# Scores in two tiles, smaller first MLP chunks, and transposes moved from TensorE to DMA from block 12 on

## The chip, the cores and the metric

The kernel runs on one core of one Trainium2 chip. The metric is device time in microseconds (us). The engines are named as in the profile: PE (TensorE matmul), PEld (its weight load), DVE (VectorE), ACT (ScalarE), POOL (GpSimd) and SP (SyncE, whose queue issues most DMAs).

## The reference, cut to what matters

```python
# q, k, v: (8, 8, 576, 64) float32; w_ch1: (512, 2048), w_ch2: (2048, 512)
scores = q @ k.transpose / sqrt(64) - slope_h * |i - j|      # only 0 <= i - j < 128, else masked
x  = softmax(scores) @ v                                     # heads side by side: (8, 576, 512)
xn = (x - mean) / sqrt(var + 1e-6) * g_ln
out = x + relu(xn @ w_ch1) @ w_ch2
```

Attention looks back over at most 127 positions. The 8 x 576 rows of x then pass through a layer norm and a two-matmul MLP with a residual.

## The kernel before, in words

The 4608 rows form 36 blocks of 128 rows. Two sequences of 576 rows are nine blocks, so block number modulo 9 says where a block lies: r = 0 has no block before it, r = 4 is half one sequence and half the next.

**Attention of a block i.** SP loads q, k and v (three DMAs, or six where a block spans two sequences) into rings of five buffers. POOL casts them to fp16 (L337, L346). PE transposes q and k in eight 128x128 pieces into one PSUM bank (task `T`, L354), and DVE copies the bank to `qkt` (L362). PE makes the scores against this block's and the previous block's keys in two halves (`Sa` and `Sb`, L380), each a group of eight matmuls into its own half of one four-bank PSUM tile, `sc`. ACT takes the exponential of each half (L403), DVE multiplies it with a table of masks and biases (L409). PE multiplies with v (`pva`, `pvb`, L423), DVE divides by the row sums into `xb` (L439, L443), takes mean and variance (L459, L464) and makes `xs` (L470). PE transposes `xs` in four pieces (`TX`, L480), and ACT or DVE copies them into `xt` (L490, L488).

**MLP of a chunk.** Four blocks are a chunk. For each of 16 groups of hidden units PE does four matmuls of 512 columns into one PSUM bank (task `A`, L519), and ACT or DVE applies the relu (L531, L529). For each block 16 matmuls of 512 columns follow (task `B`, L545), DVE adds the residual (L553) and SP stores the block (L561). Four PSUM banks, `fb`, serve T, the value products, TX, A and B in turn.

**What sets the order.** Before anything is emitted, a planner (`Plan.run`) plays the program through with a cost for each task written into the code, and the order of each engine is the order in which the planner starts its tasks. Among tasks that could start at once it takes the one with the lowest due time `v`. Attention runs 1.45 chunks ahead of the MLP (`LEAD`). On the chip each engine runs its list in that order and waits on semaphores. SP's list mixes loads and stores. A new load may not be issued before the eighth DMA ahead of it on that queue has landed (the waits on DMAHW lanes in the order).

Of the kernel before, what the change touches and what calls it, by code (L numbers as in the profile page):

```python
# [45 lines left out]
class Plan:  # L46
# [17 lines left out]
    def run(self):  # L64
# [74 lines left out]
def kernel(  # L139
# [24 lines left out]
    NCHUNK = NBLK // CB  # L164
# [40 lines left out]
    q16 = ring("q16", 3, [P, d_model], FP16)  # L205
    k16 = ring("k16", 3, [P, d_model], FP16)
# [22 lines left out]
    LEAD = 1.45  # L229

# [15 lines left out]
    def dma(name, eng, issue, secs, emit, deps=(), v=0.0):  # L246
        t = add(name + ".i", (eng, issue), emit, deps, v, lat=0.0)
        return t, add(name, ("DMA", secs), None, [t], v, lat=2.0)
# [37 lines left out]
    for dst, lst, name in ((mmix, tmix, "mmix"), (mnew, tnew, "mnew")):  # L286
        vv = av(3, 0.0) - 200
# [10 lines left out]
    tmix += [add("z1", ("POOL", 0.6), z1, list(tmix), av(3, 0.1) - 200)]  # L298
    tmix += [add("z2", ("POOL", 0.6), z2, tmix[:2], av(3, 0.1) - 200)]
    tnew += [add("z3", ("POOL", 1.2), z3, list(tnew), av(3, 0.1) - 200)]  # L300
# [10 lines left out]
    W_AFTER = {0: 4, 1: 8}  # L311
    t_w1, t_w2 = [], []
    for n in range(4):
        def emit(e, b, n=n):
            nc.gpsimd.dma_start(out=w1sb[:, :, 512 * n : 512 * n + 512], in_=w1r[:, :, 512 * n : 512 * n + 512])
        t_w1.append(dma(f"w1_{n}", "POOL", 0.9, 3.25, emit, loads[W_AFTER[0] - 1][2], av(W_AFTER[0], 0.5) - 300)[1])
    for n in range(4):
        def emit(e, b, n=n):
            nc.gpsimd.dma_start(out=w2sb[:, 4 * n : 4 * n + 4, :], in_=w2r[:, 4 * n : 4 * n + 4, :])
        t_w2.append(dma(f"w2_{n}", "POOL", 0.9, 3.25, emit, loads[W_AFTER[1] - 1][2], av(W_AFTER[1], 0.5) - 300)[1])  # L320

    qkt_done, vx_done, aggr_done, xt_done = {}, {}, {}, {}

    def attention(i):
# [5 lines left out]
        def e_cast(dst, src):  # L330
            def emit(e, b):
                en = {"POOL": nc.gpsimd, "DVE": nc.vector}.get(e)
                s = src[i][:, :, :].rearrange("p h d -> p (h d)")
                if en is None:
                    nc.scalar.activation(out=dst[i][:, :], in_=s, func=AF.Copy)
                else:
                    en.tensor_copy(out=dst[i][:, :], in_=s)  # L337
            return emit

        c_eng = {"POOL": 0.62}  # L340
        cq = add(f"cq{i}", c_eng, e_cast(q16, q32), lq, av(i, 0.0))
        ck = add(f"ck{i}", c_eng, e_cast(k16, k32), lk, av(i, 0.1))
        q32.reads(i, cq); k32.reads(i, ck); q16.writes(i, cq); k16.writes(i, ck)

        def e_cv(e, b):
            nc.gpsimd.tensor_copy(out=vx[i][:, :, 0:D], in_=v32[i][:, :, :])  # L346
        cv = add(f"cv{i}", ("POOL", 0.66), e_cv, lv_, av(i, 0.2))
        v32.reads(i, cv); vx.writes(i, cv)

        def e_t(e, b):  # L350
            pt = fb[b][:, :].bitcast(FP16).rearrange("p (a hp c) -> p a hp c", a=2, hp=HP)
            for a, s in ((0, q16), (1, k16)):
                for hp in range(HP):
                    nc.tensor.transpose(pt[:, a, hp, :], s[i][:, hp * P : hp * P + P], iden[:, :])  # L354
        tt = add(f"T{i}", ("PE", 0.48), e_t, [cq, ck, d_iden], av(i, 1.0), acq=("fb", f"T{i}"))
        q16.reads(i, tt); k16.reads(i, tt)

        def e_ev(e, b):
            src = fb[plan.held[f"T{i}"][1]][:, :].bitcast(FP16)
            dst = qkt[i][:, :, :, :].rearrange("p a hp c -> p (a hp c)")  # L360
            if e == "DVE":
                nc.vector.tensor_copy(out=dst, in_=src)  # L362
            else:
                nc.scalar.activation(out=dst, in_=src, func=AF.Copy)
        ev = add(f"ev{i}", {"DVE": 0.7}, e_ev, [tt], av(i, 1.2), rel=f"T{i}")
        qkt.writes(i, ev)
# [4 lines left out]
        def e_s(half):  # L371
            def emit(e, b):
                for slot in range(2):
                    hp = 2 * half + slot
                    for side in (() if r == 0 else (0,)) + (1,):
                        for g in range(2):
# [4 lines left out]
                                sc[:, 2 * half + g, c0 : c0 + P],  # L381
# [5 lines left out]
            return emit  # L387
# [4 lines left out]
        for half, s_ in ((0, sa), (1, sb_)):  # L392
            qkt.reads(i, s_)
            if r:
                qkt.reads(i - 1, s_)

            def e_x(e, b, half=half):
                o = probs[i][:, 2 * half : 2 * half + 2, :, lo:]
                n_ = sc[:, 2 * half : 2 * half + 2, :].rearrange("p b (s c) -> p b s c", s=2)[:, :, :, lo:]
                if r:  # L400
                    o = o.rearrange("p b s c -> p b (s c)")
                    n_ = sc[:, 2 * half : 2 * half + 2, :]
                nc.scalar.activation(out=o, in_=n_, func=AF.Exp, scale=inv_sqrt_d)  # L403
            ex = add(f"ex{'ab'[half]}{i}", ("ACT", 1.03 if r else 0.62), e_x, [s_], av(i, 2.4 + half), rel=f"S{'ab'[half]}{i}")
            probs.writes(i, ex)

            def e_m(e, b, half=half):
                pv = probs[i][:, 2 * half : 2 * half + 2, :, lo:]
                nc.vector.tensor_tensor(out=pv, in0=pv, in1=mask[:, 2 * half : 2 * half + 2, :, lo:], op=ALU.mult)  # L409
            pr.append(add(f"mk{'ab'[half]}{i}", ("DVE", 0.69 if r else 0.42), e_m, [ex] + t_mask, av(i, 3.0 + half)))  # L410
# [45 lines left out]
        c, j = i // CB, i % CB  # L456
# [17 lines left out]
        xs_ = add(f"xs{i}", ("DVE", 0.69), e_xs, [ag, d_g], av(i, 6.6))  # L474
        xs.writes(i, xs_)

        def e_tx(e, b):
            pt = fb[b][:, :].bitcast(FP16)[:, 0 : NKB * P].rearrange("p (kb c) -> p kb c", kb=NKB)
            for kb in range(NKB):
                nc.tensor.transpose(pt[:, kb, :], xs[i][:, kb * P : kb * P + P], iden[:, :])  # L480
        tx = add(f"TX{i}", ("PE", 0.26), e_tx, [xs_, d_iden], av(i, 7.5), acq=("fb", f"TX{i}"))
        xs.reads(i, tx)

        def e_xt(e, b):
            src = fb[plan.held[f"TX{i}"][1]][:, :].bitcast(FP16)[:, 0 : NKB * P].rearrange("p (kb c) -> p kb c", kb=NKB)
            dst = xt[c][:, :, j * P : j * P + P]
            if e == "DVE":
                nc.vector.tensor_copy(out=dst, in_=src)  # L488
            else:
                nc.scalar.activation(out=dst, in_=src, func=AF.Copy)  # L490
        xt_ = add(f"xt{i}", {"ACT": 0.6, "DVE": 0.45}, e_xt, [tx], av(i, 7.6), rel=f"TX{i}")
        xt.writes(c, xt_)
        xt_done[i] = xt_

        if j == CB - 1:
            ag4 = [aggr_done[c * CB + n] for n in range(CB)]

            def e_ln(e, b):
                nc.scalar.activation(out=lv[c][:, :], in_=mv[c][:, :, 1], func=AF.Ln, bias=eps_t[:, :])
# [105 lines left out]
```

## Time and profile before

| | us |
|---|---|
| median of 3 runs | 363.4 (362.27 to 363.58) |
| the profiled execution, its own time | 362.91 |
| its span, first to last instruction | 361.1 |
| PE busy | 332.4 (92%) |
| DVE busy | 216.7 (60%) |
| ACT busy | 157.5 (44%) |
| POOL busy | 78.8 (22%) |

The median and the profiled execution's time are of the whole launch; the span is what the engines' records cover. Busy time of PE counts modelled ends of pipelined matmuls. The granted TensorE clock is 1.00 throughout.

### The profile page before, as it was taken

The numbers are of one execution on the slowest core, as the hardware profiler recorded it, in microseconds if no ns is written. First come the engines' busy times: TensorE is split into PE (matmuls) and PEld (weight loads), VectorE is DVE, ScalarE is ACT, GpSimd is POOL, SyncE is SP. The second block draws the span as 40 slices with busy tenths as digits, with TensorE's granted clock in tenths as the row PEclk, the third lists the DMA queues.
The fourth block names the chain that finished last, engine by engine and source line by source line (L and its number), as shares of the span: only waits on it lengthen the run. The fifth ranks groups of instructions, "written<-read, shape, count | busy, mean of one in ns | idle before, by whom it ended". The sixth has DMA issues, their size and how long they took to land.

```text
span 361.1 us, 6732 instructions
## 1 busy us (share of the span) xinstructions
PE 332.4 (92%) x2672; PEld 173.4 (48%) x2672; DVE 216.7 (60%) x444; ACT 157.5 (44%) x237; POOL 78.8 (22%) x127
## 2 busy tenths in 40 slices
PE   1586999999999999999999999999999999999995
PEld 0364455545545545544554554555455555444442
DVE  0578497667658666666657666765676667641011
ACT  4253576245334542464245433653365335612700
POOL 4851541632112121112101211230111100000000
PEclk9999999999999999999999999999999999999999
DMA  9999999999996444564454346441000010002002
GB/s 169 226 194 212 218 196 208 201 230 224 234 186 196 93 88 124 142 115 93 122 134 93 89 118 145 119 89 56 33 29 2 29 61 31 0 31 87 0 33 86
DMA packets 122384, 42.75 MB, mean 118 GB/s; under 512 B 113392, under 2 KB 117616, under 8 KB 122352
## 3 DMA queue, kind: packets, MB, share of 16 engines
q1 hardware_dynamic: 118128, 38.12, 47.0%
q0 software_dynamic: 4224, 4.19, 7.0%
q8 instruction: 21, 0.34, 0.4%
q14 instruction: 11, 0.09, 0.1%
HBM read 37.06 MB, written 9.44 MB: 129 GB/s over the span
## 4 chain that ended last, share of the span: by engine, by line
PE 80%; ACT 12%; DVE 3%; POOL 2%; DMA 1%; issue 1%; SPq 0%; ACTq 0%; DVEq 0%
PE fb L519 32%; PE fb L545 32%; ACT probs L403 8%; PE sc L380 5%; PE fb L423 5%; PE fb L354 4%; PE fb L480 2%; ACT xt L490 2%; ACT ht L531 1%; DMA k<-in_k_dram 1%; DVE probs L409 1%; DVE xb L443 1%; POOL mmix L290 1%; POOL mnew L290 1%; DVE st L459 1%
## 5 line engine op out<-in xcount | busy, mean ns | idle before, releaser
L519 PE MATMUL fb<-xt,w1sb 128*128 128x512 f16 x576 | 140.7, 383 | 0.0
L545 PE MATMUL fb<-w2sb,ht 128*128 128x512 f16 x576 | 137.7, 379 | 0.0
L531 ACT ACTIVATE ht<-fb 128x512 f16<-128x512 f32 x118 | 70.4, 598 | 75.3 <-PE fb L519 75.1
L403 ACT ACTIVATE probs<-sc 128x1024 f16<-128x1024 f32 (+1 forms) x72 | 69.8, 974 | 37.2 <-PE sc L380 36.9
L519 PEld LDWEIGHTS <-w1sb 128*128 128x128 f16 x576 | 51.3, 98 | 52.9 <-issue 1.4
L545 PEld LDWEIGHTS <-ht 128*128 128x128 f16 x576 | 51.0, 98 | 52.3
L553 DVE SCALAR_TENSOR_TENSOR ot<-fb,rstd,xb 128x512 f32<-128x512 f32 x36 | 26.8, 748 | 46.4 <-PE fb L545 45.3
L346 POOL CAST vx<-v 128x512 f16<-128x512 f32 x36 | 22.6, 631 | 137.7 <-PE fb L423 128.9
L409 DVE TENSOR_TENSOR probs<-probs,mreg 128x1024 f16<-128x1024 f16 (+1 forms) x56 | 37.2, 666 | 24.8 <-ACT probs L403 24.4
L423 PEld LDWEIGHTS <-probs 128*128 128x128 f16 x544 | 26.9, 102 | 20.4 <-DVE probs L409 3.5
L490 ACT ACTIVATE xt<-fb 128x512 f16<-128x512 f16 x20 | 11.9, 597 | 55.1 <-PE fb L480 52.2
L337 POOL CAST q<-q 128x512 f16<-128x512 f32 x36 | 23.5, 653 | 57.1 <-issue 25.1
L380 PEld LDWEIGHTS <-qkt 64*128 64x128 f16 x544 | 19.4, 98 | 31.8 <-issue 24.7
L423 PE MATMUL fb<-vx,probs 128*128 128x65 f16 x544 | 29.9, 200 | 4.4 <-POOL vx L346 3.1
L529 DVE TENSOR_SCALAR ht<-fb 128x512 f16<-128x512 f32 x26 | 18.0, 692 | 24.1 <-PE fb L519 24.1
L380 PE MATMUL sc<-qkt,qkt 64*128 64x128 f16 x256 | 23.0, 229 | 9.4 <-ACT probs L403 6.6
L443 DVE TENSOR_TENSOR xb<-fb,rec 128x256 f16<-128x256 f32 x72 | 30.3, 423 | 2.1
L362 DVE COPY qkt<-fb 128x1024 f16<-128x1024 f16 x36 | 24.7, 686 | 10.4 <-PE fb L354 10.3
L470 DVE SCALAR_TENSOR_TENSOR xs<-xb,mv,g_t 128x512 f16<-128x512 f16 x36 | 28.3, 787 | 1.0
L380 PE MATMUL sc<-qkt 64*128 64x128 f16 x288 | 25.3, 229 | 0.8 <-DVE qkt L362 0.8
L459 DVE BATCH_NORM_STATS2 st<-xb 128x6 f32<-128x512 f16 x36 | 25.0, 694 | 1.1
L337 POOL CAST k<-k 128x512 f16<-128x512 f32 x36 | 23.0, 640 | 8.1 <-DMA k<-in_k_dram 8.0
(28 smaller groups left out, 135.8 us busy)
## 6 DMA issues: line engine op xcount, KB each, us to landing
out_dram<-ot SPq DMA_DIRECT2D x36, 256.0 KB, 2.1
q<-in_q_dram SPq DMA_DIRECT2D x32, 256.0 KB, 4.3
k<-in_k_dram SPq DMA_DIRECT2D x32, 256.0 KB, 4.6
v<-in_v_dram SPq DMA_DIRECT2D x32, 256.0 KB, 4.4
w1sb<-in_moe_w_ch_dram POOLq DMA_DIRECT2D x4, 512.0 KB, 10.9
w2sb<-in_moe_w_ch_dram POOLq DMA_DIRECT2D x4, 512.0 KB, 11.0
q<-in_q_dram SPq DMA_DIRECT2D x8, 128.0 KB, 3.7
k<-in_k_dram SPq DMA_DIRECT2D x8, 128.0 KB, 3.6
```

The source lines that it names most:

```text
L337: en.tensor_copy(out=dst[i][:, :], in_=s)
L380: nc.tensor.matmul(sc[:, 2 * half + g, c0 : c0 + P], kt[rows, 1, hp, :], qkt[i][rows, 0, hp, :], start=True, stop=True,)
L403: nc.scalar.activation(out=o, in_=n_, func=AF.Exp, scale=inv_sqrt_d)
L409: nc.vector.tensor_tensor(out=pv, in0=pv, in1=mask[:, 2 * half : 2 * half + 2, :, lo:], op=ALU.mult)
L423: nc.tensor.matmul(pp[:, hh * (D + 1) : hh * (D + 1) + D + 1], probs[i][:, bank, slot, side * P : side * P + P], vx[i - 1 + side][:, h, 0 ...
L443: nc.vector.tensor_tensor(out=xb[i][:, 256 * half : 256 * half + 256].rearrange("p (h d) -> p h d", d=D), in0=pp[:, :, 0:D], in1=rec[2 * i ...
L459: nc.vector.bn_stats(out=st[i][:, :], in_=xb[i][:, :])
L470: nc.vector.scalar_tensor_tensor(out=xs[i][:, :], in0=xb[i][:, :], scalar=mv[c][:, j, 0:1], in1=g_t[:, :], op0=ALU.subtract, op1=ALU.mult,)
L519: nc.tensor.matmul(fb[b][:, :], w1sb[:, kb, f * P : f * P + P], xt[c][:, kb, :], start=(kb == 0), stop=(kb == NKB - 1),)
L531: nc.scalar.activation(out=ht[c][:, f, :], in_=src, func=AF.Relu)
L545: nc.tensor.matmul(pm[:, :], ht[c][:, f, j * P : j * P + P], w2sb[:, f, :], start=(f == 0), stop=(f == NFB - 1),)
L553: nc.vector.scalar_tensor_tensor(out=ot[i][:, :], in0=fb[plan.held[key][1]][:, :], scalar=rstd[c][:, j : j + 1], in1=xb[i][:, :], op0=ALU. ...
```

## The change

- **Transposes by DMA.** From block 12 on q and k are cast into one tile `qk16` (a ring of four in place of two rings of three), and one DMA transpose on SP's queue writes `qkt` from it (256 KB). `xs` is transposed by a second one into `xt` (128 KB). For these 24 blocks the PE tasks T and TX and the copies behind them are gone. Blocks 0 to 11 keep them.
- **Scores as one task.** `sc` becomes two tiles, `scs[0]` and `scs[1]`, and all 16 score matmuls of a block are one task `S`.
- **Chunks.** The first two MLP chunks have two blocks, the other eight have four.
- **The start.** The copies and memsets for the special mask tables get a later due time, and the eight pieces of the weights are asked for one by one after the loads of blocks 2 to 7, instead of in fours after blocks 3 and 7.
- **The planner.** It passes over an engine for a task that another engine would finish earlier, takes DMAs first come first served, and has some costs changed.

```diff
@@ Plan.run
-                    if r is not None:
-                        cand.append((max(r, f), t.v, t, b))
+                    if r is None:
+                        continue
+                    s = max(r, f)
+                    if any(max(r, free[o]) + c < s + t.eng[e] - 1e-9 for o, c in t.eng.items() if o != e):
+                        continue
+                    cand.append((s, t.v, t, b))
...
-                c = min((c for c in cand if c[0] <= s + 1e-9), key=lambda c: c[1])
+                c = min((c for c in cand if c[0] <= s + 1e-9), key=lambda c: (c[2].v > -9e3, c[2].ready) if e == "DMA" else c[1])
@@ the chunks and the score tiles
+    CHUNKS = [2, 2] + [4] * 8
+    FIRST = [sum(CHUNKS[:c]) for c in range(len(CHUNKS))]
+    CHUNK_OF = [c for c, n in enumerate(CHUNKS) for _ in range(n)]
...
-    q16 = ring("q16", 3, [P, d_model], FP16)
-    k16 = ring("k16", 3, [P, d_model], FP16)
+    qk16 = ring("qk16", 4, [P, 2, d_model], FP16)
...
-    sc = psum.tile([P, 4, 512], FP32, tag="sc", name="sc")
+    scs = [psum.tile([P, 2, 512], FP32, tag=f"sc{n}", name=f"sc{n}") for n in range(2)]
...
-    plan.banks["sa"] = [0]
-    plan.banks["sb"] = [1]
+    plan.banks["sc"] = [0]
...
+    QK_BY_DMA = 12
+    X_BY_DMA = 12
@@ masks and weights
-        vv = av(3, 0.0) - 200
+        vv = av(2, 3.0)
...
-    W_AFTER = {0: 4, 1: 8}
+    W_AFTER = [2, 2, 3, 3, 4, 5, 6, 7]
@@ attention(i): q and k
+        if i < QK_BY_DMA:
...
+        else:
+            def e_td(e, b):
+                nc.sync.dma_start_transpose(
+                    out=qkt[i][:, :, :, :].rearrange("p a hp c -> p (a hp) c"),
+                    in_=qk16[i][:, :, :].rearrange("p a d -> p (a d)"),
+                )
+            ti, ev = dma(f"QT{i}", "SP", 1.0, 1.1, e_td, [cq, ck], av(i, -4.0))
+            qk16.reads(i, ev)
+            qkt.writes(i, ti)
@@ attention(i): scores
-        sa = add(f"Sa{i}", ("PE", 0.38), e_s(0), [ev] + prev, av(i, 2.0), acq=("sa", f"Sa{i}"))
-        sb_ = add(f"Sb{i}", ("PE", 0.38), e_s(1), [sa] + prev, av(i, 2.0), acq=("sb", f"Sb{i}"))
+        s_ = add(f"S{i}", ("PE", 0.64 if r else 0.42), e_s, [ev] + prev, av(i, 2.0), acq=("sc", f"S{i}"))
@@ attention(i): the normalised x
+        if i < X_BY_DMA:
...
+        else:
+            def e_xd(e, b):
+                nc.sync.dma_start_transpose(out=xt[c][:, :, j * P : j * P + P], in_=xs[i][:, :])
+            xi, xt_ = dma(f"XT{i}", "SP", 1.0, 0.6, e_xd, [xs_], av(i, 7.0))
+            xs.reads(i, xt_)
+            xt.writes(c, xi)
```

The order on **PE** at the scores of one steady block. Before (`sc` is the one score tile, `qkt_98` a transposed q and k, `fb_153` a PSUM bank, block 18, which has no block before it and so four matmuls in each half):

```order
L380 LDWEIGHTS qkt_98
L380 MATMUL sc<-qkt_98 128x128
L519 LDWEIGHTS w1sb
L519 MATMUL fb_153<-xt_122,w1sb 128x512
L519 LDWEIGHTS w1sb
L519 MATMUL fb_153<-xt_122,w1sb 128x512
L519 LDWEIGHTS w1sb
L519 MATMUL fb_153<-xt_122,w1sb 128x512
L519 LDWEIGHTS w1sb
L519 MATMUL fb_153<-xt_122,w1sb 128x512
L380 LDWEIGHTS qkt_98
L380 MATMUL sc<-qkt_98 128x128 [waits Activation_49]
```

Now, block 16 (`sc_147` and `sc_148` are the two score tiles; eight matmuls go to each, and the last of the first and the first of the second are shown):

```order
L401 LDWEIGHTS qkt_94
L401 MATMUL sc_147<-qkt_94 128x128
L401 LDWEIGHTS qkt_97
L401 MATMUL sc_148<-qkt_94,qkt_97 128x128
L401 LDWEIGHTS qkt_97
L401 MATMUL sc_148<-qkt_94,qkt_97 128x128
```

The four wide matmuls between the halves are gone from there, and the second half no longer waits for ACT. The first score matmul of a block from 12 on waits for a DMA instead of DVE (`L401 MATMUL sc_147<-qkt_94,qkt_97 128x128 [waits DMAHW3_49]` in block 16).

The order on **SP** around the loads of block 17. Before (`q_72`, `k_77`, `v_82` are its load buffers; a DMAHW lane is the DMA eight places ahead):

```order
L561 DMA out_dram<-ot_130 128x512 [waits DMAHW7_49,DVE_49]
L254 DMA q_72<-in_q_dram 128x8x64 [waits DMAHW0_49,Pool_49]
L254 DMA k_77<-in_k_dram 128x8x64 [waits DMAHW1_49,Pool_49]
L254 DMA v_82<-in_v_dram 128x8x64 [waits DMAHW2_49,Pool_49]
L254 DMA q_73<-in_q_dram 128x8x64 [waits DMAHW3_49,Pool_49]
L254 DMA k_78<-in_k_dram 128x8x64 [waits DMAHW4_49,Pool_49]
```

Now (`qkt_94<-qk_85` is block 12, `qkt_95<-qk_86` block 13):

```order
L261 DMA q_72<-in_q_dram 128x8x64 [waits DMAHW0_49,Pool_49]
L261 DMA k_77<-in_k_dram 128x8x64 [waits DMAHW1_49,Pool_49]
L381 DMA_TRANSPOSE qkt_94<-qk_85 128x8x128 [waits DMAHW2_49,PE_49]
L261 DMA v_82<-in_v_dram 128x8x64 [waits DMAHW3_49,Pool_49]
L261 DMA q_73<-in_q_dram 128x8x64 [waits DMAHW4_49,Pool_49]
L261 DMA k_78<-in_k_dram 128x8x64 [waits DMAHW5_49,Pool_49]
L381 DMA_TRANSPOSE qkt_95<-qk_86 128x8x128 [waits DMAHW6_49,PE_49]
```

The transposes stand among the loads of five blocks later and wait for PE, which frees the `qkt` buffer. Ahead of block 12's stand 53 loads of 256 KB (counted in whole ones) and four stores.

The order on **POOL** at the start. Before (`vx_91<-v_80` is block 0's cast of v):

```order
L337 CAST q_85<-q_70 128x512 [waits DMAHW1_49]
L337 CAST k_88<-k_75 128x512 [waits DMAHW2_49]
L290 COPY mmix<-mreg 128x1024 [waits Activation_49] x2
L290 COPY mnew<-mreg 128x1024 x2
L293 MEMSET mmix 128x8x64 [waits Pool_49]
L295 MEMSET mmix 64x8x64
L297 MEMSET mnew 64x8x128 [waits Pool_49]
L346 CAST vx_91<-v_80 128x8x64 [waits DMAHW3_49]
```

Now (`vx_89<-v_80` is that cast):

```order
L344 CAST qk_85<-q_70 128x512 [waits DMAHW1_49]
L344 CAST qk_85<-k_75 128x512 [waits DMAHW2_49]
L297 COPY mmix<-mreg 128x1024 [waits Activation_49]
L357 CAST vx_89<-v_80 128x8x64 [waits DMAHW3_49]
L297 COPY mmix<-mreg 128x1024 [waits Activation_49]
L344 CAST qk_86<-q_71 128x512 [waits DMAHW5_49]
```

One of the seven mask steps is left ahead of the cast of v; the others lie between the casts of blocks 0 to 3.

More of the change, by code (lines that the diff above doesn't have):

```diff
@@ L355, in attention @@
[L355 to L365, printed above, removed]
@@ L367, in attention, with e_s @@
         qkt_done[i] = ev
         prev = [] if r == 0 else [qkt_done[i - 1]]
-        def e_s(half):
-            def emit(e, b):
+        def e_s(e, b):
+            for half in range(2):
                 for slot in range(2):
@@ L473, in e_xs @@
             )
-        xs_ = add(f"xs{i}", ("DVE", 0.69), e_xs, [ag, d_g], av(i, 6.6))
+        xs_ = add(f"xs{i}", ("DVE", 0.75), e_xs, [ag, d_g], av(i, 6.6))
         xs.writes(i, xs_)
[L477 to L492, printed above, removed]
+        xs_done[i] = xs_
@@ L514, in mlp @@
             key = f"A{c}.{f}"
[L515 removed]
+            vm = v0 + f * per
             def e_a(e, b, f=f):
@@ L566 @@
         attention(i)
-    for c in range(NCHUNK):
+    for c in range(len(CHUNKS)):
         mlp(c)
```

149 lines of the change are left out of this document (91 added, 58 removed).

## The prediction

> **What bounds the kernel now.** I read the page's busy table first, then the windows by stage, then the chain of waits inside the steady stage, then PE's own waits. The windows (columns after the stretch: PE, PEld, DVE, ACT and POOL busy, granted clock, DMA share, GB/s):
>
> ```profile
> span 361.1 us, 6732 instructions
> PE 332.4 (92%) x2672; PEld 173.4 (48%) x2672; DVE 216.7 (60%) x444; ACT 157.5 (44%) x237; POOL 78.8 (22%) x127
> ...
> 0.00:36.00 36.00, 18.74 (x199) 13.34 (x200) 20.63 (x53) 14.37 (x23) 18.35 (x31) 1.00 1.14 200
> 36.00:108.00 72.00, 69.84 (x600) 36.59 (x598) 48.36 (x99) 34.43 (x52) 25.69 (x39) 1.00 1.09 213
> 108.00:252.00 144.00, 140.27 (x1158) 72.28 (x1156) 95.56 (x193) 67.70 (x101) 27.76 (x46) 1.00 0.46 112
> ```
>
> From 36 us on PE is busy 97% of each stretch at full clock, and DVE reaches only two thirds, so PE sets the pace. The DMA engines are full until 108 us and half idle afterwards. That split matters below. The chain of waits through one steady block, and PE's timeline at the same place:
>
> ```profile
> 182.91 0.92 ACT probs L403
> ...
> 201.38 1.03 ACT probs L403
> 202.40 0.04 issue
> 202.44 0.40 PE sc L380 x8
> 202.84 1.83 PE fb L519 x8
> 204.67 0.24 PE fb L423 x8
> ...
> 206.89 0.45 PE fb L354 x8
> 207.33 2.59 PE fb L545 x12
> 209.92 0.24 PE fb L480 x4
> ...
> 220.09 0.92 ACT probs L403
> ```
> ```profile
> 200.78 0.23 PE L380 MATMUL sc<-qkt,qkt 64*128 64x128 f16 x2
> ...
> 201.10 1.04 PE L519 MATMUL fb<-xt,w1sb 128*128 128x512 f16 x4
> 202.44 0.23 PE L380 MATMUL sc<-qkt,qkt 64*128 64x128 f16 x2 [0.30 <-ACT probs L403]
> ```
>
> One exponential per block ends in the chain, and the rows at 182.91 and 220.09 lie four blocks apart: 37.18/4 = 9.30 us per block. What PE must do in one: 12 wide matmuls in 2.59 us are 0.216 us each, and a block has 32 of them (16 at L519, 16 at L545): 6.91. The eight q and k transposes (L354) 0.45, the four of x (L480) 4 x 0.056 = 0.22, two score halves at 201.10 - 200.78 = 0.32 each, two value halves at 0.24: 8.70 in all. So 0.60 us per block is lost. Most of it is one wait. The second score half follows four wide matmuls that begin at 201.10 and need 0.86, so it could start at 201.96. It starts at 202.44, when the first half's exponential is over: 0.48 us. The two halves lie in one tile, `sc`, and in the built order the second half waits for ACT.
>
> **The change part by part.** (a) *Twelve transposes leave PE in 24 blocks (12 to 35).* 24 x (0.45 + 0.22) = 16.1 us, all on PE's path. DVE's copies of the results to `qkt` and the copies to `xt` on ACT and DVE go too.
>
> ```profile
> L362 DVE COPY qkt<-fb 128x1024 f16<-128x1024 f16 x36 | 24.7, 686 | 10.4 <-PE fb L354 10.3
> L488 DVE COPY xt<-fb 128x512 f16<-128x512 f16 x16 | 6.8, 424 | 8.6 <-PE fb L480 8.6
> L490 ACT ACTIVATE xt<-fb 128x512 f16<-128x512 f16 x20 | 11.9, 597 | 55.1 <-PE fb L480 52.2
> ```
>
>  They ran under PE's wide matmuls, so they count for nothing here; uncovered they would be 0.69 and 0.42 to 0.60 us a block.
>
> (b) *Two score tiles, and one score step.* The scores now run as 16 matmuls with no wait between the halves. The exponentials run back to back on ACT, which is busy for 67.70 of 144 us, and PE has wide matmuls to fill in. The saving is 0.48 us each time. How often?
>
> ```profile
> PE 80%; ACT 12%; DVE 3%; POOL 2%; DMA 1%; issue 1%; SPq 0%; ACTq 0%; DVEq 0%
> PE fb L519 32%; PE fb L545 32%; ACT probs L403 8%; PE sc L380 5%; PE fb L423 5%; PE fb L354 4%; PE fb L480 2%; ACT xt L490 2%; ACT ht L531 1%; DMA k<-in_k_dram 1%; DVE probs L409 1%; DVE xb L443 1%; POOL mmix L290 1%; POOL mnew L290 1%; DVE st L459 1%
> ...
> PE sc L380 <- ACT probs L403: 6.6, 22, 0.6
> ```
>
> PE's waits record it 22 times. Eight per cent of the span is about 29 exponentials of 1 us in the chain. I take 27, since two or so lie in the start where other waits rule: 27 x 0.48 = 13.0 us, bounds 10.6 and 14.
>
> (c) *The start.* POOL's mask work of 5.8 us stands before the first cast of v, and PE's first value matmul waits 3.1 us for that cast. In the new order one mask copy is ahead of it. The first MLP chunk now needs two blocks instead of four, with the weights asked for earlier.
>
> ```profile
> 6.45 2.03 POOL L290 COPY mmix<-mreg 128x1024 f16<-128x1024 f16 x2
> 8.42 2.03 POOL L290 COPY mnew<-mreg 128x1024 f16<-128x1024 f16 x2
> ...
> 11.31 0.94 POOL L297 MEMSET mnew<- 64x1024 f16 x1
> 12.21 0.60 POOL L346 CAST vx<-v 128x512 f16<-128x512 f32 x1
> ...
> PE fb L423 <- POOL vx L346: 3.1, 1, 3.1
> ...
> 34.34 1.71 PE fb L519 x4
> ...
> 343.52 13.83 PE fb L545 x64
> 357.37 0.75 DVE ot L553
> ```
>
> Split into two halves, the first chunk has 64 more matmuls of half the width; at 0.108 us each they are still longer than the 0.056 at which the x8 row above passes matmuls with their own weights, so the sum stays. Counted over the program in these durations, PE has 1152 x 0.216 + 544 x 0.04 + 544 x 0.03 + 432 x 0.056 = 311 us of matmuls before, and with 144 transposes 295 after. So 361.1 - 311 = 50 us are lost now: the tail after 357.37 is 3.7, the stage 36 to 324 holds 31 blocks at 0.60 = 18.6, and about 27.7 fall in the first 36 us. The change can win back between nothing and about 10 of these. What caps it is (d).
>
> (d) *48 DMA transposes enter SP's queue*, in line with loads and stores: 256 KB per block for q and k, 128 KB for x; each issue holds SP for about as long as the load in the last row below, so six a block stay far below 8 us. No transposing DMA is in this trace. The nearest rows:
>
> ```profile
> q1 hardware_dynamic: 118128, 38.12, 47.0%
> q0 software_dynamic: 4224, 4.19, 7.0%
> ...
> out_dram<-ot SPq DMA_DIRECT2D x36, 256.0 KB, 2.1
> q<-in_q_dram SPq DMA_DIRECT2D x32, 256.0 KB, 4.3
> k<-in_k_dram SPq DMA_DIRECT2D x32, 256.0 KB, 4.6
> ...
> 105.63 0.37 SPq L254 DMA_DIRECT2D v<-in_v_dram  x1
> ```
>
> SP's queue moves 38.12 MB in 0.470 x 361.1 = 169.7 us, or 1.17 us per 256 KB. That is the lower bound: 1.17 + 0.58 = 1.75 us of the DMA engines per block. The upper bound is a load's whole landing time with no overlap, 4.6 + 2.3 = 6.9 us. I take 1.17 and 0.58 and add a little for gaps, because a square of 128 columns has rows of 256 bytes, as a head's row in a load has. The Trainium skill, DMA: Bandwidth & Descriptors, section "Latency and other measured facts", gives 261 GB/s for such a transpose, an estimate of 1.0 us for 256 KB; no run here shows it yet.
>
> When does this bind? In the order, the transpose for block 12 stands behind 53 loads, 4 stores and all weights: 57 x 1.17 + 0.07 x 361.1 (25.3) + about 1.6 for the small tables = 93.6, plus its own 1.17, a start at about 2 us and 0.9 to report (a store lands after 2.1, of which 1.17 is transfer): 97.7 us. PE, before it comes to block 12's scores, has 128 half-wide and 172 wide matmuls, 176 for scores, 176 for values and 144 transposes: 71.4 us. With today's 27.7 of lost start and 0.1 a block it is there at about 100. The two nearly meet, so a better start buys 2 or 3 us at most; above that PE would only wait for the transpose. The same tie holds up to block 19. After that the loads thin out (0.46 of the DMA engines' time above) and each transpose may be issued once the scores of three blocks earlier are done, some 24 us before its own, so a few us of delay hide. The x transposes have more: they feed MLP chunks, of which the first is that of blocks 12 to 15.
>
> The added wait: a transpose waits on PE for a free `qkt` buffer or on DVE for `xs`, and behind it in SP's queue stand the loads of five blocks later and stores. POOL's casts and then PE wait for those, late by the same amount. I add 1 to 8 us for late transposes between blocks 12 and 19, and take 4.
>
> *Sum.* 361.1 - 16.1 - 13.0 - 3 + 4 = 333.0. A second way: scores of block 12 at 99, then 223.6 us of matmuls, 24 x 0.1, a tail of 3.7 and the 4: 332.7. The profiled execution took 362.91 us beside its span of 361.1, so 1.8 is added: **334.5 us**. Its 362.91 lies 0.5 under the median of 363.4, which I leave alone.
>
> **The rivals.** *Late queue, still faster.* The tie of (d) goes against PE: each of the 8 + 4 transposes that fall while the queue is full costs a further 1 us, about a load's share of the engines once more, if SP's queue runs dry behind each. For it speak the DMA share of 1.09 up to 108 us and a median landing of 4.3 to 4.6 us for a load, four times its transfer. Against it: the engines have half their time free soon after. 334.5 + 12 = 346 us.
>
> *Slower.* Transposes do not overlap in the queue, and each holds it for its landing time: 6.9 us a block beside 3 loads and 1 store at 4.7. Then 24 x 11.6 = 278 us from 97.7 on, and after the last x transpose the last chunk remains (4 x 6.91 + 3.7 = 31.3): 407 + 1.8 = 409 us. It decides from where 24 x (4.7 + X) exceeds 361.1 - 97.7 - 31.3 = 232 us, at X = 5.0 us a block, 2.9 times the loads' rate. For it: the trace holds no such transfer, and SP's queue is one. Against it: a load lands after 4.6 us and costs 1.17, so about four are in flight in that queue at once.
> *Slower, square by square.* The 12 squares of 128x128 of a block pass one after another, each at half the landing time of the smallest plain table of two squares:
>
> ```profile
> dist_t<-dist SPq DMA_DIRECT2D x1, 64.0 KB, 1.7
> ```
>
> 12 x 0.85 = 10.2 us a block, so 97.7 + 24 x 14.9 + 31.3 + 1.8 = 488 us. Against it: that landing is mostly latency, since 64 KB at the loads' rate is 0.29 us. The Trainium skill's page VectorE: DVE Perf Modes, section "The three transpose paths", speaks for this rival and against the change: 1309 ns for a DMA transpose of 128x128, 390 ns on TensorE, and TensorE advised. By it, an estimate, a block has 15.7 us and the time is some 620 us. This trace disagrees on TensorE, where eight take 0.45 us in a row, so I read both figures as those of one transpose alone.
>
> *No gain.* The gain of (a) and (b) is eaten by another engine. DVE has 95.56 of 144 us and loses copies, and ACT has 67.70, so this needs a cause that I do not see; the time would stay near 363 us.
>
> **How the numbers follow.** Forecast, 326 to 343 us: 0.70. Late queue, 343 to 361: 0.16. Below 326, the start worth more: 0.02. Within 0.5% of 363.4, about what a measurement here can tell from no change: 0.02. Slower: 0.10, of which 0.08 by landing times and 0.02 square by square. The range 325 to 350 holds the forecast and most of the late queue, 0.82. Faster is 0.70 + 0.16 + 0.02 = 0.88.
>
> **What would show it.** (a) L354 and L480 fall to a third of their instructions. (b) No PE wait on the exponential between score halves, and a block period near 9.30 - 0.48 - 0.67 = 8.15 us after block 20. (c) The first L519 matmul well before 34.34 us. (d) Transposes of 256 KB that take 1 to 1.5 us of the DMA engines, and PE waits on DMA of under 8 us in all, between 95 and 145 us. The forecast is wrong if PE waits for transposes beyond block 20, or if SP's queue shows holds of several us at each of them.

## The result, and the profile after

The changed kernel takes **332.83 us** (median of 4 runs, 329.89 to 333.16) against 362.95 us (median of 4 runs, 362.27 to 363.58) for the kernel before: a ratio of 0.915, 95% interval 0.910 to 0.921. Medians and ratios are of fast runs alone; one run below, 338.39 us of the kernel with one score tile, is a slow one. Predicted were 334.5 us and a range of 325 to 350. The profiled execution took 333.16 us with a span of 331.4. The total is within 2 us; the terms of the sum are not all that near, and the experiments below take them apart.

The page of the changed kernel: span, busy times, queues (packets, MB, share of 16 DMA engines), chain by engine, and the last group of the transposes that stay on PE.

```profile
span 331.4 us, 6333 instructions
PE 306.1 (92%) x2448; PEld 162.3 (49%) x2448; DVE 194.6 (59%) x409; ACT 151.1 (46%) x242; POOL 81.3 (25%) x127
...
q1 hardware_dynamic: 156528, 47.56, 70.6%
...
PE 84%; DMA 5%; DVE 4%; POOL 3%; SPq 1%; issue 1%; ACT 0%; DVEq 0%
...
L366 PE MATMUL fb<-iden,qk 128*128 128x128 f16 x96 | 9.3, 254 | 7.4 <-DMA iden<-iden 7.3
```

PE is still 92% busy of a span that is 29.7 us shorter, so PE still sets the pace. ACT's 12% of the chain is gone. The q and k transposes on PE are 96 instead of 288. SP's queue carries 9.4 MB more, and its share of the engines went from 47.0% to 70.6%. PE's waits (total, times, longest, in us):

```profile
PE fb L366 <- DMA iden<-iden: 7.3, 1, 7.3
PE fb L503 <- DVE xs L491: 5.5, 3, 2.8
PE sc L401 <- DVE qkt L374: 2.8, 5, 0.9
PE fb L443 <- DVE probs L429: 2.2, 5, 0.9
PE fb L552 <- DMA w1sb<-in_moe_w_ch_dram: 0.8, 1, 0.8
PE fb L552 <- DVE xb L463: 0.7, 1, 0.7
PE sc L401 <- ACT probs L422: 0.6, 1, 0.6
```

One wait on the exponential is left of 22, and none on a DMA transpose; PE's weight load has one of 0.3 us on a transpose. POOL does wait for them: its casts stand still 46.2 us in all until a transpose frees their `qk16` buffer, and PE feels none of it. What the transposes look like from SP (the hold of the issue, in ns, minimum, median and maximum, then first and last start) is in two groups of its queue, with the time from issue to landing under each:

```profile
L381 SPq DMA_TRANSPOSE qkt<-qk x24: 1231/1970/3177, 93.7 to 255.4; - x24
...
DMA to landing us min/median/max: 3.0/4.4/5.9
```
```profile
L518 SPq DMA_TRANSPOSE xt<-xs x24: 1189/1216/1347, 121.0 to 288.6; - x24
...
DMA to landing us min/median/max: 2.4/2.6/5.3
```

In the chain the scores of a block are now one step. The next rows are those of blocks 20 to 28:

```profile
158.64 0.55 PE sc L401 x16
...
190.85 0.55 PE sc L401 x16
191.40 5.29 PE fb L578 x24
196.69 0.49 PE fb L443 x16
197.17 1.73 PE fb L578 x8
198.90 0.55 PE sc L401 x16
...
222.60 0.55 PE sc L401 x16
```

Blocks 20 to 28 begin 63.96 us apart, 8.00 us a block. Between two scores there is only PE work. Finally the first three stages by window (columns as in the prediction), before and after:

```profile
0.00:36.00 36.00, 18.74 (x199) 13.34 (x200) 20.63 (x53) 14.37 (x23) 18.35 (x31) 1.00 1.14 200
36.00:95.00 59.00, 57.15 (x495) 29.99 (x493) 40.89 (x84) 30.93 (x46) 22.28 (x34) 1.00 1.08 216
95.00:145.00 50.00, 48.37 (x402) 25.20 (x400) 33.49 (x68) 19.77 (x29) 10.80 (x18) 1.00 0.66 145
```
```profile
0.00:36.00 36.00, 20.21 (x228) 16.30 (x228) 20.92 (x49) 16.13 (x33) 21.41 (x33) 1.00 1.10 195
36.00:95.00 59.00, 54.34 (x534) 33.35 (x535) 47.67 (x101) 28.75 (x47) 24.00 (x35) 0.97 1.07 211
95.00:145.00 50.00, 49.00 (x416) 24.81 (x414) 33.99 (x73) 23.49 (x34) 13.45 (x23) 1.00 1.21 217
```

Over these 145 us PE idles 20.7 us before and 21.5 after: the early part won no PE time. The gain is less work and fewer waits in the part behind it. The DMA engines are as full from 95 to 145 us as they were earlier (1.21, where it was 0.66).

### The profile page after: what moved, and what is told of

It is laid out like the page before. It is cut to its first block, busy times and chain, and to the rows that moved or that the text cites. A ratio compares the mean times of both kernels' runs of the same rounds, so it can differ in the third digit from the quotient of the medians.

```text
span 331.4 us, 6333 instructions
## 1 busy us (share of the span) xinstructions
PE 306.1 (92%) x2448; PEld 162.3 (49%) x2448; DVE 194.6 (59%) x409; ACT 151.1 (46%) x242; POOL 81.3 (25%) x127
## 3 DMA queue, kind: packets, MB, share of 16 engines
q1 hardware_dynamic: 156528, 47.56, 70.6%
## 4 chain that ended last, share of the span: by engine, by line
PE 84%; DMA 5%; DVE 4%; POOL 3%; SPq 1%; issue 1%; ACT 0%; DVEq 0%
PE fb L578 37%; PE fb L552 37%; PE sc L401 5%; PE fb L443 5%; DMA w1sb<-in_moe_w_ch_dram 4%; DMA k<-in_k_dram 1%; DVE probs L429 1%; PE fb L366 1%; SPq L261 1%; POOL qk L344 1%; POOL mnew L297 1%; POOL w1sb L324 1%; DVE st L480 1%; DVE qkt L374 1%; POOL vx L357 1%
## 5 line engine op out<-in xcount | busy, mean ns | idle before, releaser
L552 PE MATMUL fb<-xt,w1sb 128*128 128x512 f16 (+1 forms) x640 | 136.3, 363 | 1.7 <-DMA w1sb<-in_moe_w_ch_dram 0.8
L578 PE MATMUL fb<-w2sb,ht 128*128 128x512 f16 x576 | 131.6, 379 | 0.2 <-ACT ht L564 0.2
L564 ACT ACTIVATE ht<-fb 128x512 f16<-128x512 f32 (+1 forms) x137 | 76.7, 562 | 82.7 <-PE fb L552 82.2
L552 PEld LDWEIGHTS <-w1sb 128*128 128x128 f16 x640 | 60.3, 99 | 58.6 <-issue 1.5
L344 POOL CAST qk<-q 128x512 f16<-128x512 f32 x36 | 23.8, 662 | 87.6 <-DMA qkt<-qk 46.2
L443 PEld LDWEIGHTS <-probs 128*128 128x128 f16 x544 | 24.5, 100 | 14.6 <-DVE probs L429 4.1
L459 DVE RECIPROCAL rec<-fb 128x4 f32<-128x4 f32 x72 | 12.6, 178 | 28.6 <-PE fb L443 26.1
L562 DVE TENSOR_SCALAR ht<-fb 128x512 f16<-128x512 f32 (+1 forms) x23 | 13.4, 585 | 27.1 <-PE fb L552 26.9
L344 POOL CAST qk<-k 128x512 f16<-128x512 f32 x36 | 24.0, 667 | 5.6 <-DMA k<-in_k_dram 4.7
L401 PEld LDWEIGHTS <-qkt 64*128 64x128 f16 x544 | 16.4, 97 | 15.4 <-issue 12.5
L401 PE MATMUL sc<-qkt,qkt 64*128 64x128 f16 x256 | 18.9, 224 | 2.7 <-DVE qkt L374 2.0
L401 PE MATMUL sc<-qkt 64*128 64x128 f16 x288 | 20.5, 224 | 0.8 <-DVE qkt L374 0.8
L366 PE MATMUL fb<-iden,qk 128*128 128x128 f16 x96 | 9.3, 254 | 7.4 <-DMA iden<-iden 7.3
```

The lines of the kernel that those rows point to most:

```text
L344: en.tensor_copy(out=qk16[i][:, a, :], in_=s)
L401: nc.tensor.matmul(scs[half][:, g, c0 : c0 + P], kt[rows, 1, hp, :], qkt[i][rows, 0, hp, :], start=True, stop=True,)
L443: nc.tensor.matmul(pp[:, hh * (D + 1) : hh * (D + 1) + D + 1], probs[i][:, bank, slot, side * P : side * P + P], vx[i - 1 + side][:, h, 0 ...
L552: nc.tensor.matmul(fb[b][:, 0:n_], w1sb[:, kb, f * P : f * P + P], xt[c][:, kb, 0:n_], start=(kb == 0), stop=(kb == NKB - 1),)
L564: nc.scalar.activation(out=ht[c][:, f, 0:n_], in_=src, func=AF.Relu)
L578: nc.tensor.matmul(pm[:, :], ht[c][:, f, j * P : j * P + P], w2sb[:, f, :], start=(f == 0), stop=(f == NFB - 1),)
```

## The experiments

The steady period, read from the chain rows of the scores of blocks 20 and 28 in each kernel, is used throughout. Before, the first halves are at

```profile
173.12 0.35 PE sc L380 x8
...
246.56 0.35 PE sc L380 x8
```

so the period is 73.44/8 = 9.18 us a block. (The prediction's 9.30 is that of blocks 21 to 25; block 27, in the eight, has only half the scores.)

### Transposes back on PE

The changed kernel with both cutoffs at 36, so that no block uses a DMA transpose.

```diff
-    QK_BY_DMA = 12
-    X_BY_DMA = 12
+    QK_BY_DMA = 36
+    X_BY_DMA = 36
```

> The changed kernel with the DMA transposes undone: all 36 blocks transpose on PE again, the two score tiles, the chunks and the start are kept. Theory (the 24 x 0.67 us of transposes lay on PE's path, and the DMA side cost nothing): 333 + 16 = 349 us, block period 8.72 us. Rival 1 (the DMA queue gives part of the gain back): less than half of it is lost, 341 us or below. Rival 2 (the freed PSUM banks and copies on DVE and ACT were worth as much again): 355 us or above.

Measured: 346.71 us (345.31 to 347.8), ratio to before 0.954 (0.951 to 0.958). The DMA transposes are worth 13.9 us by the medians. The runs differ in their mean granted clock: at 0.995 the kernel here took 347.28 and 347.80 us and the changed kernel 332.69 to 333.16, at 1.000 they took 345.31 and 329.89, so at equal clock the transposes are worth 14.6 to 15.4 us. Its chain has the scores of blocks 20 and 28 at

```profile
163.98 0.55 PE sc L401 x16
...
233.29 0.55 PE sc L401 x16
```

69.31/8 = 8.66 us a block against 8.00: 0.67 us, just the 0.45 + 0.22 of the two groups of transposes. Times 24 that is 16.0, so 2.1 us of it are lost elsewhere by the medians. Both rivals fall.

### Two score tiles alone

The kernel before, its order unchanged, with `sc` cut into two tiles.

```diff
-    sc = psum.tile([P, 4, 512], FP32, tag="sc", name="sc")
+    scs = [psum.tile([P, 2, 512], FP32, tag=f"sc{n}", name=f"sc{n}") for n in range(2)]
...
-                                sc[:, 2 * half + g, c0 : c0 + P],
+                                scs[half][:, g, c0 : c0 + P],
```

> The kernel before, with its order unchanged, and only the four-bank score tile split into two tiles. Theory (the 0.48 us wait between the score halves stands in one tile for two things, and comes about 27 times on PE's path): 363 - 13 = 350 us, and no wait of PE on the exponential of the same block. Rival (the wait only moves, to the exponential of the second half or to the value products): 357 us or above.

Measured: 354.36 us (354.25 to 355.17), ratio 0.976 (0.973 to 0.979): between the theory's 350 and the rival's 357. No wait on the exponential is left among PE's waits. The chain of a steady block in this kernel:

```profile
187.31 0.33 PE sc L380 x8
187.64 0.97 PE fb L519 x4
188.61 0.33 PE sc L380 x8
188.94 1.83 PE fb L519 x8
```

The second half starts 1.30 us after the first, where it took 202.44 - 200.78 = 1.66 before: 0.36 won, not 0.48. The prediction counted on four wide matmuls at 0.86 between the halves, and behind a group of scores four of them take 0.97. The same 0.11 stands behind the second half (1.83 for eight, otherwise 1.73), and two halves of 0.33 take 0.66 where one group of 16 takes 0.55. So the period is 71.26/8 = 8.91 us (rows at 169.32 and 240.58), 0.27 below before. It is less than 0.36 since not all blocks had the long wait: of the eight before, four have their halves 1.66 or 1.67 us apart, three 1.51 or 1.52, and block 27 1.24, against 1.30 and for block 27 1.19 here.

### One score tile, scores in one step

The changed kernel with the one four-bank tile of before, and all else as changed.

```diff
-    scs = [psum.tile([P, 2, 512], FP32, tag=f"sc{n}", name=f"sc{n}") for n in range(2)]
+    sc = psum.tile([P, 4, 512], FP32, tag="sc", name="sc")
```

> The changed kernel with one four-bank score tile instead of two, the scores still one task of 16 matmuls. Theory (it is the order that counts here: no exponential stands between the halves, so nothing waits): 333 us within 2. Rival (a shared tile holds the first exponential until all 16 matmuls are done, and the next scores until both exponentials are): 0.3 us or more in each of 30 blocks, 342 us or above.

Measured: 333.51 us (332.48 to 334.86, three runs), ratio 0.918 (0.915 to 0.922), not to be told from the changed kernel. One score task removes the wait whatever the tiles are, since no exponential lies between the halves in PE's order. With the run before: either half of the edit cures the wait, and the single step also saves the 0.22 us a block of splitting. From 8.91 to the 8.66 of the kernel with PE transposes are 0.25, though these two differ in the chunks and the planner too; no run has the single step alone.

### The old start

The changed kernel with nine chunks of four blocks, the mask work early, and the weights asked for after blocks 3 and 7, as before.

```diff
-    CHUNKS = [2, 2] + [4] * 8
+    CHUNKS = [4] * 9
...
-    W_AFTER = [2, 2, 3, 3, 4, 5, 6, 7]
+    W_AFTER = [3, 3, 3, 3, 7, 7, 7, 7]
```

> The changed kernel with the start of the kernel before: chunks of four blocks from the first on, the mask steps on POOL ahead of the first cast of v, the weights asked for in fours after blocks 3 and 7. Theory (the new start won nothing, since in the trace block 12's scores come at 101.9 us, where PE's 71.4 us of matmuls and the old lost 28.9 put them): 333 us within 2. Rival (the prediction's 3 us, or more, were won at the start and lost again before block 12): 336 us or above.

Measured: 335.28 us (333.07 to 337.67), ratio 0.923 (0.917 to 0.929), between the theory's 335 and the rival's 336. The new start is worth 2.4 us by the medians, but the runs overlap, so between nothing and about 5. In its trace, which is that of its longest run, PE waits 4.7 us for DMA transposes (1.6 at scores, 3.1 at a first MLP matmul), as the changed kernel does not.

### Weights still earlier

```diff
-    W_AFTER = [2, 2, 3, 3, 4, 5, 6, 7]
+    W_AFTER = [0, 0, 1, 1, 2, 3, 4, 5]
```

> The changed kernel with the eight pieces of the weights asked for after the loads of blocks 0, 0, 1, 1, 2, 3, 4 and 5 instead of 2, 2, 3, 3, 4, 5, 6 and 7. In its trace the last of the first four pieces takes 13.2 us to land, at 32.0 us, and PE is busy for 6.2 of the 10 us from 30 to 40. Theory (the DMA engines are full from 2 us on, so weights that come earlier push loads back by as much): within 2 of 333 us. Rival (the order of weights and loads is what holds the first chunk): PE busy by 25 us, 328 us or below.

Measured: 336.6 us (333.61 to 337.89), ratio 0.925 (0.920 to 0.931): above the theory's 335, and far from the rival's 328. PE's waits now show 5.1 us on the casts of q and k, which the changed kernel does not have:

```profile
PE fb L366 <- POOL qk L344: 5.1, 4, 2.5
```

The DMA engines are full from the start (a share of 1.07 from 0 to 36 us), so it fits that a piece of the weights that comes earlier makes a load come later.

### Each transpose twice, and each followed by a plain copy

In the changed kernel each DMA transpose is issued a second time into a spare tile that nothing reads; in the second kernel a plain copy of the same bytes, in rows of 256 bytes, stands in its place.

```diff
+                nc.sync.dma_start_transpose(
+                    out=qkd[i % 4][:, :, :, :].rearrange("p a hp c -> p (a hp) c"),
+                    in_=qk16[i][:, :, :].rearrange("p a d -> p (a d)"),
+                )
```
```diff
+                nc.sync.dma_start(
+                    out=qkd[i % 4][:, :, 0:P],
+                    in_=qk16[i][:, :, :].rearrange("p a (h c) -> p (a h) c", c=P),
+                )
```

> The changed kernel with every DMA transpose issued twice, the second time into a spare tile that nobody reads; the planner is not told. The changed kernel's queue moved 64 us more of the DMA engines' time than before, 2.68 us a block, so this adds 2.68 more: 5.36. By the prediction's own bound (24 blocks x (4.7 + X), deciding from X = 5.0) it would be slower than before: 97.7 + 24 x 10.1 + 31.3 + 1.8 = 373 us. Rival (loads run far ahead and stop early, so only the whole matters: 260 us of the DMA engines now, 324 then, still under the span): PE waits only between blocks 12 and 20, 335 to 350 us.

> As the kernel with every transpose issued twice (371.7 us), but the second of each pair is a plain copy from SBUF to SBUF of the same bytes, cut into the same 256-byte rows, to a spare tile. Theory 1 (the bytes in the DMA engines decide: 1.75 us a block at the loads' rate, X = 2.68 + 1.75 = 4.4, under the bound of 5.0): 350 to 360 us, and PE waits on transposes. Theory 2 (what a transpose costs beyond a copy decides: SP is held 1.2 to 2 us by each, 0.5 by a load, and its crossbar time): 333 to 342 us.

Measured: 371.66 us (370.79 to 375.93) with the second transpose, slower than before (ratio 1.026, 1.019 to 1.032) and near the theory's 373, and 357.21 us (356.39 to 361.45) with the copy (0.986, 0.978 to 0.993), inside the first theory's 350 to 360. Span and queue of the first, then of the second, and one piece of the first one's chain:

```profile
span 374.2 us, 6378 instructions
...
q1 hardware_dynamic: 194928, 57.01, 74.3%
```
```profile
span 356.0 us, 6378 instructions
...
q1 hardware_dynamic: 194160, 57.00, 78.3%
```
```profile
159.56 3.66 DMA xt<-xs
...
163.26 16.01 PE fb L559 x60
```

The DMA time of SP's queue is 0.706 x 331.4 = 234.0 us in the changed kernel, 278.0 with the second transpose, 278.7 with the copy. So a further pair costs the engines 1.83 us a block as transposes and 1.86 as copies: the engines move a transpose like a copy, and the 1.75 of the prediction is about right for such a pair. The first pair costs more, (234.0 - 169.7)/24 = 2.68. Why is not shown; it would follow if all packets took longer in a fuller queue. The Trainium skill, Advanced Engine Details and Errata, section "X-Bar Transpose (TRN2)", says that on this chip transpose DMAs are as fast as regular ones; by the engines' time this trace agrees, 1.83 against 1.86.

By the kernel's time they are not alike: the copy costs 24.4 us, the transpose 38.8. PE's first waits, of the first and the second kernel:

```profile
PE sc L407 <- DMA qkt<-qk: 14.7, 6, 4.6
PE fb L559 <- DMA xt<-xs: 11.2, 2, 9.3
...
PE fb L559 <- DMA qkd<-qk: 6.3, 1, 6.3
```
```profile
PE sc L407 <- DMA qkt<-qk: 11.7, 5, 4.2
...
PE fb L559 <- DMA xt<-xs: 5.2, 2, 3.9
PE fb L559 <- DMA qkd<-qk: 3.3, 1, 3.3
```

The waits differ by 32.2 - 20.2 = 12 us. (Nothing reads `qkd`; who ended a wait is inferred, and these two rows are waits that the profile puts down to it.) What the second kernel does not have is the longer hold of SP: its copies hold SP for 0.62 and 0.61 us (medians, 256 and 128 KB), the second transposes for 1.31 and 1.26. That this hold makes the difference is argued, not shown; transposes could also wait for one another.

Both kernels also keep buffers longer, since the spare DMA reads `qk16` or `xs` too. POOL's longest waits for a `qk16` buffer, in the changed kernel and with the second transpose:

```profile
POOL qk L344 <- DMA qkt<-qk: 46.2, 10, 8.1
```
```profile
POOL qk L346 <- DMA qkd<-qk: 132.2, 20, 13.1
```

With the copy it is 118.7 us. The first kernel's chain runs through such waits: casts behind a spare transpose (3.26 us) and DVE's `xs` behind two (2.48 and 4.29). So the doubling tests held buffers along with the load on the queue, and these runs do not tell the two apart. And a wait can cost more than its length. In the chain piece 60 wide matmuls take 16.01 us behind a gap of 3.7, and 12.95 in the changed kernel. The granted clock of this kernel from 145 to 250 us is 0.86. So the nearness of the time to the expectation from the prediction's formula is partly chance: the formula lets the queue set the pace to the end, while PE waits only between 100 and 250 us, and a part of the loss is clock and a part may be held buffers, which the formula does not have.

### Where the cutoff may lie

The changed kernel with both cutoffs at 6, and at 16 in place of 12.

> The changed kernel with the DMA transposes from block 6 on instead of 12. PE has 6 x 0.67 = 4.0 us less to do, and the DMA queue 6 x 2.68 = 16 us more before block 12, in a stage in which its engines are full. Theory (the queue decides there: block 12's transpose lands 16 us later than 97.7, at about 114, and PE waits for the transposes of blocks 6 to 12): PE waits on transposes of about 10 us, 339 us or above. Rival (loads run far ahead and give way, so PE waits for nothing): 333 - 4 = 329 us.

> The changed kernel with the transposes of blocks 12 to 15 back on PE (cutoff 16 in place of 12). Theory (each moved transpose pair is worth what PE would spend on it, and from block 12 on nothing waits for the DMA transposes): four blocks more at 13.9 us / 24 = 0.58 us each on PE, so 332.8 + 2.3 = 335.1 us, between 333 and 338. Rival (the DMA queue is so full up to 108 us that the four early transposes cost about what they save): 332.8 or a little below, 330 to 333.

Measured: 358.7 us (356.75 to 361.61) from block 6, ratio 0.988 (0.982 to 0.994); 333.86 us (332.58 to 335.29) from block 16, ratio 0.918 (0.915 to 0.921). From block 6 on, PE's first wait and its window from 36 to 95 us are

```profile
PE sc L401 <- DMA qkt<-qk: 18.9, 5, 7.1
```
```profile
36.00:95.00 59.00, 33.44 (x318) 21.41 (x319) 28.04 (x60) 17.85 (x31) 17.73 (x29) 0.79 1.04 209
```

While the loads fill the queue a transpose comes late here, PE is busy for 33.44 of 59 us, and what it does there is at a clock of 0.79. From block 16 the time rises by 1.0 us where four blocks of 0.58 would have made 2.3. The median lies within the theory's bounds, but the difference from the changed kernel is smaller than these runs can tell. Whether the move pays at blocks 12 to 15 is therefore not shown.

### Fewer loads ahead of the transposes

The changed kernel with three buffers each for q, k and v in place of five, so that loads run two blocks less ahead; and the same with the cutoffs at 8.

```diff
-    q32 = ring("q32", 5, [P, H, D], FP32)
+    q32 = ring("q32", 3, [P, H, D], FP32)
```

> The changed kernel with three q, k and v buffers in place of five, so that the loads ahead of a transpose in SP's queue are those of two blocks fewer (6 x 1.17 = 7 us of DMA engines). Theory (the queue's fill matters only in the first 100 us, where PE waits for no transpose as it is): the block 12 transpose lands some 7 us earlier, near 91 us, PE does not need it before 101.9, and the time stays at 332.8, between 331 and 335. Rival (the loads that run far ahead stretch everything behind them, the transposes as well as the stores, and cost PE time): 326 to 330. Second rival (with two blocks less of lead the loads themselves come late): PE waits on casts, 336 or more.

> The changed kernel with three q, k and v buffers and the transposes by DMA from block 8 on (cutoff 8). PE reaches the scores of block 8 at 69.6 us in the changed kernel. Behind 53 loads the block 12 transpose landed at 98; with cutoff 8 and five buffers 41 loads stand ahead, 14 us less, so about 84, which is 14 us late (with cutoff 6 PE waited 18.9 us and the time was 358.7). Theory (what makes an early transpose late is the loads ahead of it in the queue): three buffers take 6 loads or 7 us away, so it is there near 77, PE waits some 7 us once, pays half of it again in clock, and gains 4 x 0.58 = 2.3: 332.8 + 7 + 3 - 2 = 341 us, between 337 and 346. Rival (it is the bytes of the DMA engines in the first 100 us, not the order in the queue): as late as with five buffers, about 350 us or more.

Measured: 331.44 us (331.23 to 331.74), ratio 0.911 (0.910 to 0.913), with three buffers; 345.01 us (341.5 to 346.14), ratio 0.947 (0.942 to 0.952), with three and cutoff 8. The first transpose of block 12 in SP's queue, in the changed kernel and with three buffers:

```profile
93.67 1.80 SPq L381 DMA_TRANSPOSE qkt<-qk  x1
```
```profile
82.91 2.19 SPq L381 DMA_TRANSPOSE qkt<-qk  x1
```

It is issued 10.8 us earlier, and the time barely moves, since PE did not wait for it. Three buffers are the shortest median of all kernels here and the steadiest, but the interval lies within that of the changed kernel, so it is not shown to be faster. With cutoff 8 the time fell where the theory had it, though not by its wait: block 8 finds its transpose in time, and PE waits at blocks 13 and 14 (1.58 and 3.46 us) and runs from 95 to 145 us at a clock of 0.83. That loads ahead in the queue are what makes a transpose late is supported by the earlier issue, but cutoff 8 with five buffers was not run.

### Only x by DMA

```diff
-    QK_BY_DMA = 12
+    QK_BY_DMA = 36
```

> The changed kernel with q and k transposed by PE in all blocks, and only the normalised x by DMA from block 12 on (128 KB a block). Theory (each transpose moved is worth its PE time and nothing waits for the DMA): x is 0.22 of 0.67 us, a third of the 13.9 us between 346.7 and 332.8, so 342.1 us, between 340 and 344. Rival (the transposes of x also took the copies from ACT and DVE, and these cost PE banks and waits): x worth more than its third, 336 to 339.

Measured: 340.99 us (340.09 to 342.12), ratio 0.938 (0.935 to 0.940). The x transposes bring 5.7 of the 13.9 us, where their third would be 4.6, within the theory's bounds; q and k bring 8.2. The queue's time, 0.553 x 338.7 = 187.3 us here and 0.488 x 343.5 = 167.6 with all transposes on PE, gives 0.82 us of the engines for an x transpose and, up to the 234.0 of the changed kernel, 1.95 for one of q and k. The prediction had 0.58 and 1.17.

## Why the prediction was right

The ladder, by medians of the runs: before 363.0, two tiles alone 354.4, everything but the DMA transposes 346.7, all 332.8. The same by the steady block: 9.18, 8.91, 8.66, 8.00 us.

**(a) Transposes off PE: right.** 0.67 us a block were predicted and 0.67 measured between the steady periods. Of the 16.1 us 13.9 arrive by the medians, 14.6 to 15.4 at equal clock.

**(b) The wait between the halves: kind right, price too high, and a second gain missed.** "The saving is 0.48 us each time", times 27 gave 13.0 with bounds 10.6 and 14. Taking the wait away alone brought 9.1 us, below the lower bound. The step that failed is the start of the second half at 201.96: it left out the 0.11 us that PE loses behind a group of scores, and it took the wait of block 23 for that of every block, where three of eight have 0.15 less. On the other side the sum had nothing for making one step out of two, which saves two such pieces, 0.22 a block, or 27 x 0.22 = 5.9 us. That figure is worked out from rows, not measured alone; the 354.4 - 346.7 = 7.7 us between the two kernels hold it and the new start's 2.4 together. The two errors nearly cancel, which is luck: 9.1 + 5.9 = 15.0 against 13.0.

**(c) The start: right in size, not in kind.** -3 was predicted, 2.4 measured, between 0 and 5. The tie that was to cap it is there: the transpose for block 12 is issued at 93.67, so with the median landing of 4.4 it is there at 98.1 (97.7 predicted), and PE comes for it at 101.9 (about 100). But the first part did not get shorter: the first L552 matmul runs at 22.56, where the first L519 matmul ran at 34.15, and then PE stands still for `xs` and, in the profiled run, pays it again in clock:

```profile
32.02 1.92 PE L552 MATMUL fb<-xt,w1sb 128*128 128x256 f16 x16 [0.85 <-DMA w1sb<-in_moe_w_ch_dram]
...
37.66 0.40 PE L503 MATMUL fb<-iden,xs 128*128 128x128 f16 x4 [2.79 <-DVE xs L491]
...
38.81 3.32 PE L552 MATMUL fb<-xt,w1sb 128*128 128x256 f16 x16
```

Sixteen matmuls of the same form take 1.92 us before that wait and 3.32 behind it (granted clock 0.74 from 40 to 45 us).

**(d) Late transposes: overpriced.** +4 was added for PE's waits between blocks 12 and 19. PE has no such wait at all. The 2.1 us that (a) does not deliver are the most that (d) can have cost, and at equal clock it is 0.7 to 1.5. The step that failed is "I add 1 to 8 us for late transposes": PE came 4 us after the transpose, not before it. The margin is thin, since in the trace with the old start PE did wait 4.7 us. The engines' time was priced too low as well: 2.68 us a pair for 1.75, and their share is 1.21 from 95 to 145 us and 0.80 from 145 to 250 instead of half their time free. The issue's hold, "about as long as the load in the last row below", was too low too: 1.97 us (median, q and k) against 0.37 in that row and 0.60 to 0.80 for the loads here. Both were harmless, as PE did not wait.

Sum: 361.1 - 13.9 - 15.0 - 2.4 = 329.8 for a span of 331.4. So the total was right since (b) as a whole was 2 us too small, (d) 4 us too large, and (a) lost 2 on the way; the 1.6 that remain are within the spread of the runs. That the end is met within 2 us is in part luck. The first sum's 333.0 would give 334.8; the 334.5 is the second way's 332.7 with 1.8. That way too has two errors: the scores of block 12 come at 101.9 us, not 99, and what follows takes 229.5 us, not 233.7.

**The rivals.** No gain: DVE (59% busy) and ACT (46%) took nothing back. Late queue: PE waits for no transpose, and the queue does not run dry (the share of 1.21). Landing times: it needed X = 5.0 us a block, and the measured cost is 1.8 to 2.7. Still it was a right place to look: a second transpose on each makes the kernel slower than before, though held buffers may have a part in that. Square by square: 12 squares of a block land in 4.4 and 2.6 us, not 10.2. The figure that spoke for it, 1309 ns a square on the Trainium skill's page VectorE: DVE Perf Modes, section "The three transpose paths", would be the price of one alone; no run here moves one alone.

## What to carry to other kernels

Where PE sets the pace, a transpose on it is paid nearly in full, and one by DMA costs the engines no more than a copy of its bytes. Begin it late enough to be there when PE comes: from block 6 on it was not. Doubling it shows how near the next bound is, but look whether the second one also holds a buffer, as it did here. Between two parts of work on one PSUM tile look for the wait, but also for the switch: joining the parts was worth 0.22 us a block beyond the wait, by the rows. A wait of PE of some us can cost more than it shows, since PE's clock may fall after it.

## What the runs showed of the hardware

- **PE's clock after a wait.** Behind a gap of 2.79 us sixteen matmuls of one form took 1.7 times as long (1.92 and 3.32 us). From the last matmul that is no transpose to the next it is 3.8 us. It does not happen each time: at the same place the kernels with one score tile and with three buffers have gaps of 2.27 and 2.28 us and then take 3.02, and those with PE transposes and from block 16 have 2.31 and 2.28 and take 1.92. In windows with waits for transposes the granted clock was 0.79 (from block 6), 0.83 (three buffers, from block 8) and 0.86 (second transpose). The Trainium skill, TensorE: Matmul & The Clock Gate, section "HAM oscillation — how this bites in real kernels", describes the same, a half clock after a wait of some us on DMA, and names 3.4 us as the gap to avoid; this trace agrees in kind, behind a wait on DVE.
- **A DMA transpose holds SP.** The median is 1.97 us for 256 KB and 1.22 for 128 KB in the changed kernel, where the loads' medians are 0.60 to 0.80 and a plain copy's is 0.62. Size alone does not set it: the shortest holds are 1.23 and 1.19, and with three buffers the median for 256 KB is 1.30.
- **A pause behind the score matmuls.** Four wide matmuls take 0.97 us behind a group of score matmuls, which use 64 rows of the array, and 0.86 behind value matmuls or transposes: 0.11 us for each group. That the change of rows is the cause is not shown.
